# Cached attention with a dense layer, one decode step: K and V of the third step in halves, FFN and part of the output projection in column tiles, unused products in loops

## The chip, the core and the metric

The kernel runs on one core of a Trainium2 chip, in one launch. The metric is the device time of one execution in microseconds (us); of several executions the median counts. A core has a matrix engine (TensorE, PE in the profile; its weight loads are PEld), VectorE (DVE), ScalarE (ACT), GpSimd (POOL) and SyncE (SP), which here issues nearly all DMA transfers. Sixteen DMA engines move the data from HBM to on-chip memory. Engines wait for one another with semaphores.

## The reference

```python
x = A_x                                   # [2, 1, 512], bf16
xn = _layernorm(x)
q = (xn @ wq) -> [2, 32, 1, 128]          # wq [512, 4096]
scores = einsum("bhqd,bhkd->bhqk", q, k_cache) * 128 ** -0.5    # k_cache [2, 32, 8192, 128]
p = softmax(scores)
o = einsum("bhqk,bhkd->bhqd", p, v_cache) # v_cache [2, 32, 8192, 128]
attention = o -> [2, 1, 4096] @ wo        # wo [4096, 512]
ffn = maximum(xn @ w1, 0) @ w2            # w1 [512, 1792], w2 [1792, 512]
return x + attention + ffn
```

(The arrows stand for reshapes.) The inputs are bf16. The two caches hold 268 MB, the weights 12 MB; each element is used once. Two rows of x are all that is multiplied with them.

## The kernel before

The 64 pairs of batch and head are worked on four at a time, in 16 steps (`NP`). A step has one tile of K and one of V, each 128 partitions by 32,768 bf16 elements, 8.39 MB. There is one buffer for each, `ks` and `vs`. A partition holds 256 rows of the cache (`KB`) of one pair; four pairs share the 128 partitions.

In each step TensorE does the following. It transposes the 256 blocks of K (128 by 128), in 32 groups of eight (L275). Each group goes into one of four PSUM tiles `tp` and is copied by VectorE or ScalarE into `kT` (L429). Then come 256 small products of `kT` with the four queries `q4` (L282), which give the scores in `Sc`. VectorE finds a maximum for each half of them (L476, L483), with help of two small products (`turn`, L294, and `spread`, L300). ScalarE makes the exponentials `prm` and their sums (L550). Then come 256 products of V with `prm` (L335), here called PV. After that TensorE runs `WARM` = 24 products whose results nobody uses (L346), in the steps 0 to 13.

The order of the loads is written out by hand on SyncE (L184 to L188): K of step t, V of step t, K of step t+1, and so on. A tile is loaded when its buffer is free: K of the next step after the last transpose of this one (semaphores `pT`), V of the next step after the last product with this V (`sW`). For steps named in `KSPLIT` and `VSPLIT` the tile comes as two DMAs of half the columns, each of which waits only for its own half of the buffer:

```python
c = slice(i * SLOT // 2, (i + 1) * SLOT // 2) if split else slice(0, SLOT)
sp.dma_start(tile[:, c], src[rows, c]).then_inc(d[i], 16)
...
KSPLIT = (0, NP - 1)
VSPLIT = (1, NP - 1)
```

Each half has its own semaphore, `dK[0]` and `dK[1]`, `dV[0]` and `dV[1]`. Where a tile comes whole, GpSimd waits for the first and raises the second (L239). wq lies in `vs` before V, and the query path (layer norm, L254 to L264) runs ahead of the loop.

After the last transpose of the last step, SyncE loads w1, w2 and wo into `ks` (L190 to L194), wo in four pieces of 18, 8, 4 and 2 of its 32 rows (`cuts`; a "row" is here 128 partitions by 512 columns). The tail after the loop is this. TensorE sums the softmax denominators (L356, fp32). It adds x into an accumulator `fin` of 128 partitions by 8 (L362). It forms the FFN's hidden layer in 56 products with two columns, w1 being the stationary operand (L373). VectorE scales and adds the two halves of PV (L494 to L512). TensorE rearranges them (L385, L389), and VectorE copies the result to `OX` (L522). Then `project` (L400) adds w2 times the hidden layer in 56 products and wo times `OX` in 128, all into `fin`, each with w2 or wo as the stationary operand and two moving columns. Each piece of wo is waited for. The end is a copy, a transpose (L420), a copy and the store.

## Time and profile before

| what | value |
|---|---|
| median of 5 executions | 660.07 us (659.49 to 660.3) |
| the profiled execution | 660.29 us |
| its span, first to last instruction | 658.4 us |
| TensorE products busy | 594.6 us, 90% of the span |
| TensorE weight loads busy | 537.3 us, 82% |
| VectorE / ScalarE busy | 261.9 us, 40% / 290.9 us, 44% |
| DMA moved | 280.66 MB, mean 426 GB/s |
| mean granted TensorE clock | 0.98 |

The profile is of one execution. The span leaves out 1.9 us that the time of that execution has besides. All points in time are us from the span's start. The "chain that ended last" is followed back from the last instruction: at each step to whatever released it. "DMA" in it is a wait for a load, from its issue to its landing. An engine's busy time is no measure of what bounds the kernel; the unused products alone make TensorE 74.8 us busier.

### The profile page before, as it was taken

Reading aid. Unit: us, or ns where it says so; the run is one execution under the profiler, and the core shown is the slowest. Engines: PE = TensorE matmul, PEld = TensorE weight load, DVE = VectorE, ACT = ScalarE, POOL = GpSimd, SP = SyncE. Lnnn points to the kernel's source line nnn. Section 1 sums busy time; section 2 is a strip of 40 time slices with the busy share of each in tenths; the row PEclk is TensorE's granted clock in tenths of the full one; section 3 lists DMA queues with packets and bytes.
Section 4 is the critical chain, followed back from the end, with each engine's and each line's share of the span. In section 5 each row is a group of like instructions: output and inputs, shape, how many; then the busy total and the mean of one; then the engine's idle time right before and its main releaser. Section 6 shows DMA issues by size and latency. Waiting matters only on the chain.

```text
span 658.4 us, 27600 instructions
## 1 busy us (share of the span) xinstructions
PE 594.6 (90%) x12987; PEld 537.3 (82%) x12987; DVE 261.9 (40%) x503; ACT 290.9 (44%) x532; POOL 7.1 (1%) x30
## 2 busy tenths in 40 slices
PE   1886999999999999999989999998999999999997
PEld 0585887988879798887969878796987879798986
DVE  1440351716235071633507153260715416071721
ACT  1332443636345263543527354353735435372820
POOL 2000000000000000000000000000000000000000
PEclk9988999989999999999999999999999999999996
DMA  9999999999999999999999999999999999999996
GB/s 380 445 440 428 403 446 402 434 446 442 418 426 434 442 442 414 434 438 442 426 422 430 446 442 434 418 426 446 442 438 418 422 446 442 442 414 417 436 420 268
DMA packets 6223, 280.66 MB, mean 426 GB/s; under 512 B 706, under 2 KB 708, under 8 KB 964
## 3 DMA queue, kind: packets, MB, share of 16 engines
q1 hardware_dynamic: 6208, 280.50, 98.9%
q8 instruction: 8, 0.13, 0.1%
q14 instruction: 3, 0.02, 0.0%
q10 hardware_dynamic: 4, 0.00, 0.0%
HBM read 280.50 MB, written 0.00 MB: 426 GB/s over the span
## 4 chain that ended last, share of the span: by engine, by line
DMA 53%; PE 44%; issue 1%; DVE 1%; SPq 0%; ACT 0%; ACTq 0%
DMA ks<-in_A_k_cache_dram 49%; PE tp L275 34%; DMA ks<-in_A_wo_dram 4%; PE ot L335 4%; PE Sc L282 4%; PE ms L346 2%; DVE mcol L476 1%; SPq L194 0%; ACT L429 0%; PE ms L294 0%; ACT kT L429 0%; PE ms L300 0%; SPq L191 0%; SPq L182 0%; SPq L170 0%
## 5 line engine op out<-in xcount | busy, mean ns | idle before, releaser
L429 DVE COPY kT<-tp 128x1024 bf16<-128x1024 bf16 x320 | 209.3, 688 | 249.2 <-PE tp L275 243.6
L275 PEld LDWEIGHTS tp<-identb,ks 128*128 128x128 bf16 x4096 | 230.4, 98 | 24.7 <-DMA ks<-in_A_k_cache_dram 22.6
L275 PE MATMUL tp<-identb,ks 128*128 128x128 bf16 x4096 | 233.4, 220 | 17.5 <-DMA ks<-in_A_k_cache_dram 16.0
L429 ACT COPY kT<-tp 128x1024 bf16<-128x1024 bf16 x192 | 188.2, 1014 | 129.5 <-PE tp L275 129.5
L282 PE MATMUL Sc<-q,kT 128*128 128x64 bf16 (+8 forms) x4096 | 133.8, 191 | 3.1 <-issue 3.1
L335 PE MATMUL ot<-prm,vs 128*128 128x64 bf16 x4096 | 131.9, 193 | 3.0 <-issue 3.0
L282 PEld LDWEIGHTS Sc<-q,kT 128*128 128x128 bf16 x4096 | 129.3, 98 | 4.5 <-issue 3.2
L335 PEld LDWEIGHTS ot<-prm,vs 128*128 128x128 bf16 x4096 | 128.0, 98 | 4.9 <-issue 3.1
L346 PE MATMUL ms<-identb 128*128 128x512 bf16 x336 | 74.8, 379 | 0.0
L476 DVE TENSOR_REDUCE mcol<-Sc 32x1 bf16<-32x128 f32 x128 | 37.0, 289 | 93.1 <-PE Sc L282 91.7
L550 ACT ACTIVATE prm<-Sc,nm 32x128 bf16<-32x128 f32 x128 | 69.0, 539 | 5.4
L545 ACT COPY nm<-ms 128x4 f32<-128x4 f32 x32 | 5.2, 163 | 139.3 <-PE ms L300 139.3
L346 PEld LDWEIGHTS ms<-identb 128*128 128x128 bf16 x336 | 31.9, 98 | 36.4
L561 ACT COPY OTf<-ot 128x8 f32 x16 | 2.7, 166 | 72.4 <-PE ot L335 72.4
L550 ACT ACTIVATION_READ_ACCUMULATOR prm<-Sc,nm x128 | 32.1, 251 | 0.0
L294 PE MATMUL ms<-identb,mcol 128*1 128x128 bf16 x32 | 6.9, 217 | 22.1 <-DVE mcol L476 22.1
L429 ACT ACT_TABLE_LOAD x16 | 20.5, 1283 | 3.6 <-issue 3.5
L294 PEld LDWEIGHTS ms<-identb,mcol 128*1 128x1 bf16 x32 | 2.5, 79 | 23.9 <-issue 23.1
L254 PE MATMUL ot<-vs,xz 128*16 128x512 bf16 x32 | 9.0, 451 | 8.8 <-DMA vs<-in_A_wq_dram 8.8
L254 PEld LDWEIGHTS ot<-vs,xz 128*16 128x16 bf16 x32 | 3.2, 102 | 14.1 <-issue 11.5
L483 DVE TENSOR_REDUCE mx<-ms 1x4 bf16<-1x128 bf16 x32 | 8.9, 278 | 13.7 <-PE ms L294 13.7
L236 POOL COPY q<-qb 128x4 bf16<-128x4 bf16 x16 | 3.0, 186 | 592.0 <-PE Sc L282 573.0
(61 smaller groups left out, 47.5 us busy)
## 6 DMA issues: line engine op xcount, KB each, us to landing
ks<-in_A_k_cache_dram SPq DMA_DIRECT2D x4, 4096.0 KB, 23.0
vs<-in_A_v_cache_dram SPq DMA_DIRECT2D x4, 4096.0 KB, 22.0
vs<-in_A_wq_dram SPq DMA_DIRECT2D x1, 4096.0 KB, 12.3
ks<-in_B_w_dram SPq DMA_DIRECT2D x2, 1792.0 KB, 16.5
ks<-in_A_wo_dram SPq DMA_DIRECT2D x1, 2304.0 KB
ks<-in_A_wo_dram SPq DMA_DIRECT2D x1, 1024.0 KB, 26.4
ks<-in_A_wo_dram SPq DMA_DIRECT2D x1, 512.0 KB, 27.2
ks<-in_A_wo_dram SPq DMA_DIRECT2D x1, 256.0 KB, 27.3
```

Source lines behind the costliest of these rows:

```text
L236: g.tensor_copy(q4[:], qb[:, U * t:U * t + U]).then_inc(sQ1, 1)
L254: i = pe.matmul(qp, lhsT=xz[:, kt, Z - g * Bsz:Z - g * Bsz + QG * Bsz], rhs=vs[:, (kt * QG + g) * 512:(kt * QG + g + 1) * 512], start=(g = ...
L275: t = pe.transpose(tp[e % 4][:, i, :], ks[:, kk * Dh:(kk + 1) * Dh], identb[:])
L282: t = pe.matmul(Sc[:, U * kk:U * (kk + n)], lhsT=kT[e][:, i, :], rhs=rep(q4[:], n), start=True, stop=True,)
L294: pe.transpose(trp[:, i * P:(i + 1) * P], mcol[:, i:i + 1], identb[:]).then_inc(sT, 1)
L335: t = pe.matmul(oh[:, i, :], lhsT=vs[:, kk * Dh:(kk + 1) * Dh], rhs=rep(prm[:, kk, :], REP), start=(first == 0), stop=(first == KB // 2 - 1),)
L346: pe.matmul(ms[:], lhsT=identb[:], rhs=identb[:].rearrange("p (o k) -> p o k", o=1).to_broadcast([P, 4, P]), start=True, stop=True,)
L429: fn(kT[e][:], tp[e % 4][:]).then_inc(kR[e % HG], 1)
L476: m = v.tensor_reduce(out=mcol[own, i:i + 1], in_=S[own, i * KB // 2:(i + 1) * KB // 2, u], axis=AX.X, op=ALU.max,)
L483: v.tensor_reduce(out=mx[:, i, :], in_=trp[:, i * P:(i + 1) * P].rearrange("o (u m) -> o u m", u=U), axis=AX.X, op=ALU.max, negate=True,). ...
L545: a.copy(nm[:, i, :], bc[:, i, :]).then_inc(sN, 1)
L550: x = a.activation(out=prm[own, k, u], in_=S[own, k, u], func=ACTF.Exp, bias=nm[own, i, u:u + 1], scale=1.0, accum_out=RS[own, i, bass.ds( ...
```

## The change

It has three parts.

1. `KSPLIT` and `VSPLIT`: K and V of step 2 (the third) come in halves. V of the last step comes whole.
2. The FFN and the first 18 rows of wo are turned around. The weights are now the moving operand, 512 columns at a time, and the stationary operand has 32 columns, of which two hold data and the others zeros or what happens to lie there and isn't used. The result takes 32 partitions, so four such products fill different 32-partition strips (`CT` = 32, `TC` = 4) of one PSUM tile. The hidden layer `hp` is made in 16 products instead of 56. ScalarE copies it to bf16, four transposes turn it, and VectorE applies the ReLU. w2 takes 14 products instead of 56, the 18 rows of wo 18 instead of 72. The four strips of the sum `y` are copied to `ys` in fp32, and four fp32 products with `sel2` (a 0/1 matrix) add them into `fin`. The other 14 rows of wo go as before; the pieces are now 18, 6, 6 and 2 rows.
3. The unused products stand in loops of five: 20 in step 0, none in step 1, 25 in the steps 2 to 13.

```diff
-WARM = 24
+CT = 32
...
-    cuts = (0, 18, 26, 30, WJ)
+    cuts = (0, 18, 24, 30, WJ)
+    WIDE = 1
-    KSPLIT = (0, NP - 1)
-    VSPLIT = (1, NP - 1)
+    KSPLIT = (0, 2, NP - 1)
+    VSPLIT = (1, 2)
...
+        g.memset(hT[:], 0.0).then_inc(sI, 1)          # GpSimd, before the loop
...
+        g.wait_ge(sS, 2 * NP)                         # GpSimd, after the loop
+        g.memset(OX, 0.0).then_inc(sI, 1)
...
+        def warm(n):
+            with pe.Fori(0, n):
+                for i in range(5):
+                    pe.matmul(ms[:], lhsT=identb[:], rhs=..., start=True, stop=True)
...
             with pe.If_lt(reg, NP - 1):
-                for i in range(WARM):
-                    pe.matmul(ms[:], lhsT=identb[:], rhs=..., start=True, stop=True)
+                with pe.If_ne(reg, 2):
+                    warm(4)
+                    with pe.If_ne(reg, 1):
+                        warm(1)
...
-        for j in range(FJ):
-            for kt in range(KT):
+        for kt in range(KT):
+            for c in range(TC):
                 i = pe.matmul(
-                    hp[:, j, :],
-                    lhsT=w1_v[:, kt, j, :],
-                    rhs=xz[:, kt, Z:Z + Bsz],
+                    tile(hp, c),
+                    lhsT=xz[:, kt, Z:Z + CT],
+                    rhs=w1_v[:, kt, first_j[c]:first_j[c] + QW, :],
...
+        pe.matmul(
+            tile(y, 0), lhsT=identb[0:Bsz, 0:CT], rhs=xsb[:], start=True, stop=False
+        )
...
+        pe.wait_ge(sF, 2)
+        for i in range(QW):
+            t = pe.transpose(tp[3][:, i, :], hb[:, i * P:(i + 1) * P], identb[:])
+        t.then_inc(sF, 1)
...
         for j in range(FJ):
-            project(w2_sb, j, hT)
+            c = j % TC
+            pe.matmul(
+                tile(y, c), lhsT=hT[:, slot[j], :], rhs=w2_sb[:, j, :],
+                start=(0 < j < TC), stop=False,
+            )
         pe.wait_ge(sV, 110)
-        for c in range(NC):
-            pe.wait_ge(*piece[c])
-            for j in range(cuts[c], cuts[c + 1]):
-                t = project(wo_sb, j, OX, j == WJ - 1)
+        for i in range(WIDE):
+            pe.wait_ge(*piece[i])
+            for j in range(cuts[i], cuts[i + 1]):
+                t = pe.matmul(
+                    tile(y, j % TC), lhsT=OX[:, j, :], rhs=wo_sb[:, j, :],
+                    start=False, stop=(j >= cuts[WIDE] - TC),
+                )
+        t.then_inc(sH, 1)
+        for i in range(WIDE, NC):
+            if i == WIDE:
+                pe.wait_ge(sF, 5)
+                for k in range(KT):
+                    pe.matmul(
+                        fin[:, k * Bsz:(k + 1) * Bsz],
+                        lhsT=ys[:, k * P:(k + 1) * P],
+                        rhs=sel2[:],
+                        start=(k == 0),
+                        stop=False,
+                    )
+            pe.wait_ge(*piece[i])
+            ...                                       # 14 rows, four products each, as before
...
+        v.wait_ge(sF, 3)                              # VectorE
+        v.wait_ge(sI, 4 + U)
+        v.tensor_scalar(out=hT[...], in0=tp[3][...], scalar1=0.0, scalar2=None, op0=ALU.max).then_inc(sF, 1)
...
+        v.wait_ge(sH, 4)
+        v.tensor_copy(ys, y).then_inc(sF, 1)
...
+        a.wait_ge(sF, 1)                              # ScalarE, at the end
+        a.copy(hb, hp).then_inc(sF, 1)
```

## The prediction

> **What bounds the kernel now.** I read the page's DMA queues first, then the chain that ended last, then the tail's timeline and the landings in the trace (sixteen per load, one for each DMA engine; I quote the last).

> ```profile
> q1 hardware_dynamic: 6208, 280.50, 98.9%
> q8 instruction: 8, 0.13, 0.1%
> ```

> The queues are full: 280.50 MB can't move faster than the stream runs. From step 3 on one 8.39 MB tile lands every 19.36 us and a step is 38.70 us. So gains can come only from the start, from holes in the stream, and from what follows the last landing.

> ```profile
> 69.59 5.18 PE ms L346 x24
> 74.77 14.31 PE tp L275 x256
> 89.08 0.01 issue
> 89.09 23.36 DMA ks<-in_A_k_cache_dram
> ...
> 146.25 5.18 PE ms L346 x24
> 151.43 0.03 issue
> 151.45 14.48 PE tp L275 x256
> 165.93 0.02 issue
> 165.95 24.19 DMA ks<-in_A_k_cache_dram
> ...
> 627.41 27.32 DMA ks<-in_A_wo_dram
> 654.73 0.05 issue
> 654.78 0.39 PE Sc L400 x8
> ```

> The chain (start, duration) shows a hole. K of the third step (K2) is issued at 89.09, when all of K1 is transposed, and the second half of V1 lands at 92.34: a lead of 3.25 us. K2 lands at 112.46, 20.12 after V1, so 0.77 beyond 19.36. In later steps the lead is 4.85 (K issued 165.95, V landing 170.80) and costs nothing. So the need lies between; 3.25 + 0.77 = 4.02 is my estimate.

> ```profile
> 650.50 2.06 PE L400 MATMUL Sc<-OX,ks 128*128 128x2 bf16 x72 [0.22 <-DMA ks<-in_A_wo_dram]
> 652.91 0.93 PEld L400 LDWEIGHTS Sc<-OX,ks 128*128 128x128 bf16 x32 [0.43 <-DMA ks<-in_A_wo_dram]
> ```

> In the tail TensorE waits for each piece of wo. The first lands at 650.37 on one engine, 649.56 on the next latest: an instruction packet (q8) sat on an engine from 646.99 for 1.07 us. The end is thus 654.73 plus 3.7 us of product, copies, store and closing, span 658.4. The profiled execution took 660.29, the median 660.07, so I add differences to the median.

> **Halves of K2 and V2.** K2's first half is issued after sixteen groups of K1: warm-up products are now 20 in step 0 (0.86 less), transposes start at 73.9, half of 14.31 later is 81.1, and the second half goes at 88.2. V1 lands at 92.34, so the hole goes: -0.77. Two more issues on SyncE (0.33 to 0.44 each) find it waiting. V2's halves are issued at about 102 and 106, with K2 landing until 111.7: nothing. V15 goes back to one load, after all of PV14 (609.6, before 605.7 for its first half); K15 lands until 615.97, so no hole, but PV15, which began at 634.85, must wait for 635.41: +0.5 for TensorE. The w1 issue behind it waits for 625.1 anyway. GpSimd forwards V15's semaphore and no longer K2's and V2's; it idles 592 us before its copies.

> **Where that stall goes.** Step 1 has no warm-up now. K2's first half lands at 102.1, PV1 ends at about 106.1, TensorE goes straight on; with the table load on ScalarE in the way this takes 15.5 as for K15 (609.6 to 625.1), to 121.9. Then 17.9 of scores and PV (89.08 to 106.97) to 139.8, and 25 products of 0.215 to 145.2. K3 can't land before 111.70 + 38.72 = 150.4: 5 us idle. After pauses of 2.5 to 3 us this trace grants half clock:

> ```profile
> 33.00:34.50 1.50, 0.55 (x9) 0.55 (x10) 0.00 (x0) 0.00 (x0) 0.00 (x0) 0.97 1.41 612
> 34.50:36.00 1.50, 1.50 (x17) 1.50 (x15) 0.50 (x1) 1.01 (x1) 0.00 (x0) 0.50 0.30 131
> 36.00:37.50 1.50, 1.50 (x17) 1.50 (x16) 0.88 (x2) 0.29 (x1) 0.00 (x0) 0.50 1.51 655
> 37.50:39.00 1.50, 1.50 (x27) 1.50 (x26) 0.78 (x2) 1.25 (x2) 0.00 (x0) 0.89 0.30 131
> ```

> (Columns: stretch, length, TensorE, weight load, VectorE, ScalarE, GpSimd, clock, DMA share, GB/s.) 17 transposes per 1.5 us instead of 27 to 30; the 128 took 8.95 instead of 7.24, so 1.71 is lost. In step 3 that makes K4's lead 4.85 - 1.71 = 3.14, and the need of 4.02 then costs 0.88. Ends: 0 (the clock stays) to 1.7 (cold twice as long). I take 0.88, by the K2 row; net of the first hole +0.1. The stall moves by two steps.

> **Loops for the unused products.** Steps from 2 on run 25, not 24: 0.215 more, under a wait of 16.0 us in 13 (1.2 a step) for K. Each pass of a loop costs the sequencer ten instructions and a jump; 48 such instructions were issued in 1.84 us, a taken branch is recorded with 0.20, a register operation with 0.07, so 0.7 against 1.08 us of five products: hidden. Were it not, up to 0.2 a pass still fits the wait; beyond, every step would be late. [...]

> **Shorter code.** TensorE ran dry at 48.43 after 961 of its records and at 62.69 after 1473: 512 records for two 16 KB packets, so edges at 1728, 1984, 2240. The code has 2,234 records. Of the products 4+56+56+72 go and 1+16+4+14+18 come, and eight passes for the fp32 four (L356 shows x8 for four): 127 pairs, 254 records, and some 20 from the loops: about 1,961, under 1984. Before, two packets came in the tail. If none comes, the first wo piece lands at 649.56 and the last at 653.85: -0.8. If one is fetched ahead anyway: 0. I take -0.8.

> **Column tiles.** Their price is open. The nearest row:

> ```profile
> L254 PE MATMUL ot<-vs,xz 128*16 128x512 bf16 x32 | 9.0, 451 | 8.8 <-DMA vs<-in_A_wq_dram 8.8
> ```

> These followed each other every 0.43 us at half clock and 0.215 at full clock, all in one column group, weight loads (102 ns) hidden. Four groups together can't beat a quarter of that; one after another they would take all of it. I take side by side, since all four differ in columns: per group five of the 18 wo products, 1.25 us with the pipeline at full clock, 2.3 at half. [...]

> The tail from PV15 (643.4 with its 0.5): fp32 sums 1.07, FFN products to 645.6 or 646.4, ScalarE's copy 0.6 (half of the 1.01 for 1024 columns), four transposes, ReLU at 648.0, w2 until 649.0 or 650.0. Before, w2 began at 648.63. New waits: TensorE waits for ScalarE's copy, with the products for OX queued behind, VectorE for the transposes, with OX's copy queued behind its ReLU (OX 648.3, before 648.97), and TensorE for the copied sum, with all later wo pieces queued behind: that one is on the path and stands in the sum below. So the wo products begin at 649.7 (649.56 + 0.1), or 650.0 at half clock. Then: products 1.25 / 2.3, copy of 512 fp32 columns 0.68 (L458) + 0.1, fp32 products 1.07 (L356) + 0.1, and 56 products of 28.6 ns (2.06 / 72) = 1.6. Sum 4.8 / 5.85, end at 654.5 / 655.85; the last landing alone would allow 653.95 + 0.44. Before it was 655.17. So -0.7 at full clock, +0.7 at half. The tail from 645.4 ran at half clock before; the wide products are just what raises the clock. Middle: 0.

> Hidden by their covers: the reduction for sel2 (0.2 us ahead of the statistics; the q path waits until 13.28, 8.4 us), memsets on GpSimd (0.5 and 0.95, idle until 24.1 and after 633).

> **Forecast: no change within 0.2% (1.3 us, about what a measurement of this kernel can tell), 0.45.** 660.07 + 0 = 660.0; own range 658.8 to 661.3.

> **Rivals.**
> Faster, 0.27: K4 finds its lead (clock restored in time), so -0.77 and 0.2 of V2's late landing stay, the code packets vanish (-0.9), full clock: 658.3. For it: both holes are real rows. Against: 5 us idle ahead of K3.
> Slower, 0.13: column tiles run one after another. FFN 16 x 0.215 = 3.4, w2 3.0, wo 3.9: the chain ends at 659.9, +4.7, 664.8; at half clock 672. It decides from a speed-up below about three at half clock, two at full. For: no row shows two at once. Against: disjoint columns.
> Slower, 0.15: all does as said, but the packet stays on the wo load, the tail is cold, and K4's lead loses 1.7 (net +0.9): products begin at 651.3, + 5.85 = 657.2, +2.0: 662.1.

> **How the numbers follow.** Faster 0.27, same 0.45, slower 0.28. The range from 658.2 to 662.4 leaves out the serial tiles (0.13) and some edges.

> **What would show it.** K2 landing at 111.7, half clock about 150 with K3's transposes near 16 us, K4 landing 20.2 after V3; no or one q8 packet after 640; eighteen wo products in 1.3 to 2.3 us, and the chain ending in L-lines of the fp32 products rather than in DMA. Wrong, if wide products start 0.2 us or more apart, if TensorE no longer waits for K in steps 5 to 13, or if K4 lands on time.

## The result, and the profile after

The changed kernel is slower, by little: 661.0 us median of 40 runs (659.83 to 664.75) against 659.63 us of 78 runs of the kernel before. The ratio is 1.0024, 95% [1.0015, 1.0032], so some 1.6 us (the medians alone give 1.4); that is just over 0.2%, though the interval reaches below it. The forecast was no change, 660.0 us; 661.0 lies inside its range of times, but against the kernel before the change is larger than the 0.2% it allowed.

The two profiled executions don't show the difference: 660.22 us after, 0.8 below its kernel's median, and 660.29 before, 0.7 above; both have a span of 658.4. They do show where time was won and given back. The page of the profile after, the DMA queue of instructions:

```profile
q8 instruction: 7, 0.11, 0.1%
```

One packet of 16 KB fewer, but one of the seven still starts at 647.62, during the load of wo.

The chain that ended last, after (start, duration; around K of the fourth step, K3, and then the tail):

```profile
122.39 28.18 DMA ks<-in_A_k_cache_dram
150.56 0.05 issue
150.61 17.28 PE tp L289 x256
...
205.48 23.54 DMA ks<-in_A_k_cache_dram
...
609.75 25.71 DMA vs<-in_A_v_cache_dram
...
644.64 3.77 PE tp L389 x16
...
649.75 1.04 PE tp L425 x14
650.79 1.10 PE tp L433 x18
651.91 0.70 DVE kT L576
652.66 1.05 PE Sc L442 x8
653.71 1.47 PE Sc L452 x56
```

K3's transposes take 17.28, where before they took 14.48. From the landing of V15 the chain is now TensorE and the copies between its products to the end, not the DMA of wo.

The timeline after, around step 2 and K4's issue (the bracket is the idle time ahead of a group):

```profile
140.07 5.56 PE L321 MATMUL ms<-identb 128*128 128x512 bf16 x25
150.61 17.28 PE L289 MATMUL tp<-identb,ks 128*128 128x128 bf16 x256 [4.99 <-DMA ks<-in_A_k_cache_dram]
167.92 0.33 SPq L193 DMA_DIRECT2D ks<-in_A_k_cache_dram  x1
```

The windows after (stretch, length, TensorE, weight load, VectorE, ScalarE, GpSimd, clock, DMA share, GB/s):

```profile
148.00:150.50 2.50, 0.00 (x0) 0.00 (x0) 0.00 (x0) 0.00 (x0) 0.00 (x0) 0.84 1.09 472
150.50:154.00 3.50, 3.39 (x32) 3.39 (x33) 1.30 (x2) 1.01 (x1) 0.00 (x0) 0.50 0.99 431
154.00:157.50 3.50, 3.50 (x43) 3.50 (x42) 1.51 (x4) 2.03 (x2) 0.00 (x0) 0.64 0.95 412
```

Before, in the middle one of these stretches (K3 began at 151.45):

```profile
150.50:154.00 3.50, 3.48 (x51) 2.75 (x49) 1.40 (x3) 1.56 (x2) 0.00 (x0) 1.00 0.78 337
```

After the change TensorE is idle for 4.99 us, and the clock is halved from 149.7 to 156.5, which is two stretches of 3.41. So K4 goes out at 167.92, only 1.99 ahead of the last landing of V3 at 169.91; before, the lead was 4.85.

| last landing, us | before | after |
|---|---|---|
| K2 | 112.46 | 111.78 |
| K3 | 151.40 | 150.56 |
| K4, after V3 | 19.34 | 20.05 |
| V4, after K4 | 19.34 | 19.74 |
| V15 | 635.41 | 635.47 |
| 18 rows of wo | 650.37 | 650.39 |
| last piece of wo | 654.73 | 654.76 |

The 0.84 won by K3 is given back entirely at K4 and V4 (0.69 + 0.38). From there on the stream is within 0.3 us of where it was.

### The profile page after: what moved, and what is told of

Its sections match the earlier page's. It is cut to its first block, busy times and chain, and to the rows that moved or that the text cites. A ratio compares the mean times of both kernels' runs of the same rounds, so it can differ in the third digit from the quotient of the medians.

```text
span 658.4 us, 27499 instructions
## 1 busy us (share of the span) xinstructions
PE 592.1 (90%) x12844; PEld 532.5 (81%) x12844; DVE 262.8 (40%) x505; ACT 291.5 (44%) x533; POOL 8.6 (1%) x32
## 3 DMA queue, kind: packets, MB, share of 16 engines
q1 hardware_dynamic: 6352, 280.50, 98.8%
HBM read 280.50 MB, written 0.00 MB: 426 GB/s over the span
## 4 chain that ended last, share of the span: by engine, by line
DMA 54%; PE 44%; DVE 1%; ACT 0%; issue 0%; SPq 0%; ACTq 0%
DMA ks<-in_A_k_cache_dram 50%; PE tp L289 32%; PE ot L358 5%; DMA vs<-in_A_v_cache_dram 4%; PE Sc L296 4%; PE ms L321 1%; PE tp L389 1%; DVE mcol L523 1%; PE Sc L452 0%; ACT L470 0%; PE tp L433 0%; PE ms L308 0%; PE Sc L442 0%; PE tp L425 0%; ACT kT L470 0%
## 5 line engine op out<-in xcount | busy, mean ns | idle before, releaser
L289 PEld LDWEIGHTS tp<-identb,ks 128*128 128x128 bf16 x4096 | 233.2, 99 | 26.5 <-DMA ks<-in_A_k_cache_dram 23.8
L289 PE MATMUL tp<-identb,ks 128*128 128x128 bf16 x4096 | 236.3, 221 | 19.5 <-DMA ks<-in_A_k_cache_dram 17.1
L321 PE MATMUL ms<-identb 128*128 128x512 bf16 x320 | 71.2, 379 | 0.0
L321 PEld LDWEIGHTS ms<-identb 128*128 128x128 bf16 x320 | 30.4, 98 | 34.7
```

The costliest lines, as they stand in the source:

```text
L289: t = pe.transpose(tp[e % 4][:, i, :], ks[:, kk * Dh:(kk + 1) * Dh], identb[:])
L321: pe.matmul(ms[:], lhsT=identb[:], rhs=identb[:].rearrange("p (o k) -> p o k", o=1).to_broadcast([P, 4, P]), start=True, stop=True,)
```

## The experiments

Each ratio is against 35 runs of the kernel before on the same chip (medians 660.19, 659.93 and 659.94 us on the three chips used). The first four share a chip: one half of the change, the other half, the suspected idle time filled in the changed kernel, and the same idle time made in the kernel before.

**loop_part_only**: the kernel before with parts 1 and 3 of the change, and its own tail.

```diff
-    KSPLIT = (0, NP - 1)
-    VSPLIT = (1, NP - 1)
+    KSPLIT = (0, 2, NP - 1)
+    VSPLIT = (1, 2)
-                for i in range(WARM):
-                    pe.matmul(ms[:], ...)
+                with pe.If_ne(reg, 2):
+                    warm(4)
+                    with pe.If_ne(reg, 1):
+                        warm(1)
```

> Before with the halves of K2 and V2, V15 whole, and the unused products in loops (20, none, 25); the tail stays as before. Theory 1, the stall that moved to the fourth step costs the time: this is about as slow as the full change, ratio to before 1.002, and K4 lands 20 us or more after V3 (19.36 would be the stream). Theory 2, the new tail costs it: this is no slower than before, ratio 0.999 to 1.000. Theory 3, V15 as one load costs it (0.5 us at PV15): the last wo piece lands no later than before and the end is about 0.1% later.

Measured: 661.4 us, ratio 1.0018 [1.0006, 1.0029]. Its timeline:

```profile
138.38 5.56 PE L306 MATMUL ms<-identb 128*128 128x512 bf16 x25
150.42 16.51 PE L274 MATMUL tp<-identb,ks 128*128 128x128 bf16 x256 [6.48 <-DMA ks<-in_A_k_cache_dram]
```

K4 is issued at 166.96 and lands 20.88 after V3, 1.52 too late. Half the change is enough for the loss. The stream isn't all of it in this execution: the last piece of wo lands at 655.11, 0.4 later than before, but the chain ends at 656.39, 1.2 later, because TensorE ran late. PV of the last step starts later than before (first line: before) and finds half clock from 636.0 to 639.4:

```profile
634.85 1.14 PE L335 MATMUL ot<-prm,vs 128*128 128x64 bf16 x32
636.19 1.89 PE L343 MATMUL ot<-prm,vs 128*128 128x64 bf16 x32 [0.42 <-DMA vs<-in_A_v_cache_dram]
```

Half clock there is in tail_part_only and step2_filled too (granted clock 0.67 and 0.64 from 634 to 638), which are no slower than before, so it alone isn't the cause; what it adds when the stream is late stays open.

**tail_part_only**: the changed kernel with the splits and the 24 unrolled products of before, so part 2 alone.

```diff
-    KSPLIT = (0, 2, NP - 1)
-    VSPLIT = (1, 2)
+    KSPLIT = (0, NP - 1)
+    VSPLIT = (1, NP - 1)
-                with pe.If_ne(reg, 2):
-                    warm(4)
-                    with pe.If_ne(reg, 1):
-                        warm(1)
+                for i in range(24):
+                    pe.matmul(ms[:], ...)
```

> Before with the new tail alone (FFN and 18 rows of wo in column tiles, pieces 18, 6, 6, 2); splits and the 24 unrolled unused products as before. Theory 1: ratio 0.998 to 1.000, since one instruction packet fewer comes in the tail. Theory 2: ratio 1.002, with the chain ending in the FFN products, the copy of the sum and the fp32 products, and not in the DMA. Its wide w1 products should again take 0.9 us per four (3.8 us in all), w2 and wo 0.215 per four at full clock.

Measured: 659.93 us, ratio 1.0001 [0.9989, 1.0013], span 658.4, one packet in the tail at 647.3. The tail neither gains nor loses. Here K2 lands only 0.31 late (before's profile: 0.77), with the same splits as before.

**step2_filled**: the changed kernel with 20 more unused products in step 2, so that TensorE stays busy until K3 lands.

```diff
                     with pe.If_ne(reg, 1):
                         warm(1)
+                    with pe.If_eq(reg, 3):
+                        warm(4)
```

> The changed kernel with 20 more unused products in step 2, 45 instead of 25, which reach to where K3 lands. Theory 1: the clock stays at full speed at K3, its transposes take 14.5 instead of 17.3 us, K4 is issued 2.8 us earlier and lands 19.4 after V3 instead of 20.05; all later landings come 0.7 to 1.1 us earlier, ratio to before 0.999 to 1.000 (from 1.0024). Theory 2: the landings move as said but the end stays, ratio 1.002.

Measured: 660.14 us, ratio 0.9999 [0.9989, 1.0009]. The windows and the timeline of it:

```profile
150.50:154.00 3.50, 3.45 (x62) 3.46 (x63) 2.10 (x4) 2.47 (x3) 0.00 (x0) 1.00 0.95 412
```

```profile
138.65 9.87 PE L321 MATMUL ms<-identb 128*128 128x512 bf16 x45
150.55 14.47 PE L289 MATMUL tp<-identb,ks 128*128 128x128 bf16 x256 [2.02 <-DMA ks<-in_A_k_cache_dram]
```

62 transposes in 3.5 us, not 32; the clock is full, K3's transposes take 14.47 again, and K4 lands 19.35 after V3. Twenty products that compute nothing take the loss away, with the new tail and V15 as one load still in place, so neither of these is the loss by itself. The last landing comes 1.5 us earlier than in the changed kernel (653.22), but this execution doesn't get that: V15 is one load, PV15 ran at half clock from 635.1 to 638.5, and the chain of the tail ended at 655.45.

**step2_cold**: the kernel before, without its 24 unused products in step 2 and otherwise untouched.

```diff
+                with pe.If_ne(reg, 3):
                     for i in range(WARM):
                         pe.matmul(ms[:], ...)
```

> Before, without the 24 unused products in step 2 alone: TensorE waits 5 to 6 us for K3 there and nothing else changes. Theory 1: half clock at K3, its transposes take 16 to 17.3 us, K4 lands up to 1 us late, ratio 1.001 to 1.002, with a wider spread of times. Theory 2: the transposes are slower but the lead of K4 (4.9 us) still covers it, ratio 1.000.

Measured: 661.65 us, ratio 1.0023 [1.0008, 1.0037]. Its timeline:

```profile
150.35 16.66 PE L275 MATMUL tp<-identb,ks 128*128 128x128 bf16 x256 [6.36 <-DMA ks<-in_A_k_cache_dram]
167.03 0.33 SPq L182 DMA_DIRECT2D ks<-in_A_k_cache_dram  x1
```

K4 lands 21.47 after V3, 2.1 late, and the last piece of wo at 655.80. So idle time ahead of K3 (6.36 us here) costs as much as the measured loss without any other part of the change.

The others ask whether a version can keep K2's gain and be faster than the kernel before.

**filled_v15_halves**: step2_filled, and V15 in halves again.

```diff
-    VSPLIT = (1, 2)
+    VSPLIT = (1, 2, NP - 1)
```

> The changed kernel with 20 more unused products in step 2 and V15 in halves again. If V15 as one load is what holds the tail (theory 3), PV15 starts about 0.5 us earlier and the last chain ends 0.5 us earlier: ratio 0.998 to 0.999. If the tail is held by the chain from the FFN products on, whatever V15 does (theory 2 within a stream that no longer stalls): PV15's end moves by less than 0.3 us and the ratio is 0.999 to 1.000.

Measured: 659.58 us, ratio 0.9996 [0.9983, 1.0008]; no difference from the kernel before. In its profiled execution 45 products didn't keep the clock:

```profile
138.43 9.87 PE L321 MATMUL ms<-identb 128*128 128x512 bf16 x45
150.46 16.09 PE L289 MATMUL tp<-identb,ks 128*128 128x128 bf16 x256 [2.15 <-DMA ks<-in_A_k_cache_dram]
```

With 2.15 us of idle the clock fell (151.4 to 154.8) and K4 came 1.15 late. With 2.02 in step2_filled it stayed, but so it did with 2.14 in filled_w1_near and in filled_old_tail (both below), which have the same 45 products; this is filled_old_tail:

```profile
150.52 14.47 PE L274 MATMUL tp<-identb,ks 128*128 128x128 bf16 x256 [2.14 <-DMA ks<-in_A_k_cache_dram]
```

So it isn't the length of the idle time that parts them; the last section works out what does.

**filled_w1_near** and **filled_w1_row**: the same, with w1's and w2's rows laid out so that the moving columns of a w1 product lie 2 elements apart (`b` = 2) or next to each other (`b` = 1) instead of 14. w2 then comes in pieces of 2 KB or 1 KB.

```diff
-        sp.dma_start(w2_sb, B_w2.rearrange("(p j) n -> p j n", j=FJ))
+        sp.dma_start(
+            w2_sb.rearrange("p (a b) n -> p a (b n)", b=b),
+            B_w2.rearrange("(a p b) n -> p a (b n)", b=b, p=P),
+        )
...
-        w1_v = w1_sb.rearrange("p kt (f j) -> p kt j f", j=FJ)
+        w1_v = w1_sb.rearrange("p kt (a f b) -> p kt a b f", b=b, f=P)
...
-                    rhs=w1_v[:, kt, first_j[c]:first_j[c] + QW, :],
+                    rhs=w1_v[:, kt, first_j[c] // b:(first_j[c] + QW) // b, :, :],
```

> As filled_v15_halves, with another order of the hidden layer: w1's moving columns lie 2 elements apart instead of 14, and w2 is loaded in 2 KB pieces instead of 14 KB. If the 0.9 us per four wide w1 products come from the distance of the columns, they take 0.22 to 0.45 per four here and the chain before the wo products shortens by 1.9 to 2.7 us; the end is then given by the last landing, 1 to 1.5 us earlier: ratio 0.997 to 0.998. If it comes from something else (the four strips of one bank, the loads), they stay at 0.9 and the ratio is as in filled_v15_halves. If the 2 KB pieces slow the load, w2 takes longer than 4.3 us from w1's landing and eats the gain.

> As filled_w1_near, with w1's moving columns next to each other and w2 loaded in 1 KB pieces. By the distance theory 0.215 per four, as w2's and wo's products; the load of w2 is the open price, 4.3 us (none) to 6 us.

Measured: 661.84 us, ratio 1.0028 [1.0014, 1.0042], and 662.68 us, 1.0046 [1.003, 1.0063]: slower than filled_v15_halves, though the w1 products became 3.5 times faster. The timeline of filled_w1_near:

```profile
642.95 1.09 PE L394 MATMUL tp<-ks,xz 128*32 128x512 bf16 x16
649.20 1.26 PE L438 MATMUL tp<-ks,kT 128*32 128x512 bf16 x18 [2.10 <-DMA ks<-in_A_wo_dram]
651.24 1.87 PE L447 MATMUL Sc<-sel,kT 128*128 128x2 f32 x8 [0.78 <-DVE kT L581]
```

What TensorE saves in the hidden layer it waits for wo (2.10), and after that wait the clock is half: the fp32 products take 1.87 instead of 1.05. (This execution, 660.01 us, is the fastest of its twelve.) w2 takes 4.71 us to load (5.21 with 1 KB), not 4.28. In filled_w1_row's execution TensorE waits 1.56 for wo, but the clock stays full in these products, and it is the slowest kernel of all:

```profile
653.46 1.05 PE L447 MATMUL Sc<-sel,kT 128*128 128x2 f32 x8 [0.78 <-DVE kT L581]
```

So half clock in the last products isn't all that makes these kernels slower.

**w1_row_w2_as_before** parts the order of w1's columns from w2's pieces: filled_v15_halves with w1's columns adjacent and w2 loaded as before.

```diff
-                    rhs=w1_v[:, kt, first_j[c]:first_j[c] + QW, :],
+                    rhs=w1_sb[:, kt, first_j[c] * P:(first_j[c] + QW) * P],
```

> As filled_v15_halves, with w1's moving columns next to each other and w2 loaded as before (the hidden layer's order is then mixed up: the FFN's sum is not the reference's). It tells apart why the versions with the other order of the hidden layer were slower. If the small pieces of w2 cost it: ratio 0.997 to 0.999 here, the wide w1 products at 0.215 per four. If it is the idle TensorE that follows short FFN products (half clock in the last products): ratio 1.002, as in filled_w1_near.

Measured: 661.57 us, ratio 1.0026 [1.0012, 1.004], about 2.0 above filled_v15_halves. So w2's pieces aren't needed for the loss. The timeline:

```profile
644.80 1.05 PE L391 MATMUL tp<-ks,xz 128*32 128x512 bf16 x16
650.87 1.26 PE L435 MATMUL tp<-ks,kT 128*32 128x512 bf16 x18 [1.93 <-DMA ks<-in_A_wo_dram]
652.91 1.86 PE L444 MATMUL Sc<-sel,kT 128*128 128x2 f32 x8 [0.78 <-DVE kT L578]
```

The same wait and the same half clock: 0.8 of the 2.0 is seen here. The 18 rows of wo also land 0.45 later than in filled_v15_halves (650.73, 650.28). The rest stays open.

**filled_old_tail** and **filled50_old_tail**: loop_part_only with V15 in halves and 45 or 50 products in step 2, so K2's gain with the old tail.

```diff
-    VSPLIT = (1, 2)
+    VSPLIT = (1, 2, NP - 1)
+                    with pe.If_eq(reg, 3):
+                        warm(4)          # warm(5) for 50
```

> Before with the halves of K2 and V2 and the loops, 20 more unused products in step 2, V15 in halves, and the tail of before: the stalls are gone, the tail is unchanged. The landings come as in step2_filled, 1 to 1.5 us before those of before. If the old tail follows its DMA, ratio 0.998; if two instruction packets in the tail and the PE chain hold it, 0.999 to 1.000, no better than the new tail.

> As filled_old_tail with 50 unused products in step 2 instead of 45, so that they reach K3's landing even when step 2 runs early. Theory 1 (the clock at K3): half clock at K3 becomes rarer, K4 lands 19.4 after V3; ratio 0.998 to 0.999 and a narrower spread. If 45 was enough already: as filled_old_tail, 0.999.

Measured: 659.60 us, ratio 0.9992 [0.9976, 1.0007], and 659.48 us, 0.9998 [0.9982, 1.0013]. K4 lands 19.34 and 19.35 after V3, and the last piece of wo at 653.30 and 653.12; the profiled spans are 657.8 and 657.3, against 658.4. With the next kernel's 657.4 these are the three shortest, yet the intervals hold 1. Both intervals lie below that of the changed kernel.

**filled50_v15_halves**: filled_v15_halves with 50.

> As filled_v15_halves with 50 unused products in step 2; there the profiled run still fell to half clock at K3. Theory 1: K3's transposes 14.5 us, K4 19.4 after V3, ratio 0.998 to 0.999.

Measured: 660.33 us, ratio 1.0011 [1.0, 1.0022], though the profiled span is 657.4 and K4 is in time (19.34). No better than the old tail.

**k2_halves_alone**: the kernel before with one edit.

```diff
-    KSPLIT = (0, NP - 1)
+    KSPLIT = (0, 2, NP - 1)
```

> Before with K of the third step in halves and nothing else: V15 in halves, 24 unrolled unused products in every step, so the hole ahead of K2 is closed and no new wait is made. If the hole is as large as in the profiled run (0.77 us), ratio 0.999; K2 lands 19.4 after V1. If the hole varies from run to run (0 to 0.8), 0.9995 to 1.000.

Measured: 660.19 us, ratio 1.0002 [0.9985, 1.0019]. Its timeline:

```profile
142.81 5.34 PE L346 MATMUL ms<-identb 128*128 128x512 bf16 x24
150.33 16.09 PE L275 MATMUL tp<-identb,ks 128*128 128x128 bf16 x256 [2.17 <-DMA ks<-in_A_k_cache_dram]
```

K2 lands 19.43 after V1, so the hole of 0.77 is gone, and the time doesn't move. Even with step 1's unused products in place, TensorE is now early in step 2 (2.17 idle) and the clock falls, so this run doesn't show the gain by itself. K4, issued 3.18 ahead, landed in time in this execution.

## Why the prediction was wrong, point by point

**The step that failed is the balance of the stream: "net of the first hole +0.1".** Its mechanism was right and is shown from both sides: idle ahead of K3, half clock, K4 issued late, a hole (step2_cold makes it, 1.0023; step2_filled removes it, 0.9999). Both terms were mis-sized.

- The gain, -0.77, was one execution's. The same K2 load, whole as before, was late by 0.31 in tail_part_only and by nothing in step2_cold. k2_halves_alone removes it for a ratio of 1.0002, with a cold K3 of its own; filled_old_tail and filled50_old_tail, with K3 warm in their profiles, come to 0.9992 and 0.9998. By the traces it was worth some 0 to 0.8, and I booked the top.
- The cost, 0.88, came from a lead of 3.14 and one cold stretch of 1.71. Measured: 2.80 more in the transposes (two cold stretches), K4's lead 1.99, and 0.69 + 0.38 late; 1.52 in loop_part_only and 2.1 in step2_cold. My upper end, "1.7 (cold twice as long)", lies among these; the value I took lies below all of them. Two cold stretches is what the prediction put at the end of its span and not into its sum.
- "Need 4.02" isn't a number of the chip: a lead of 4.20 cost 0.31 (tail_part_only), 3.25 cost 0.77, 3.19 cost 1.15 (filled_v15_halves), 3.18 cost nothing (k2_halves_alone), 2.62 cost 2.1, 1.99 cost 1.07 over two loads. So the same lead, close to the predicted 3.14, cost nothing or 1.15. The sixteen landings of K4 lie 1.93 us apart in the profile before (188.21 to 190.14) and 0.75 in the one after (189.21 to 189.96); what part that has I didn't separate.

A cost of 1.1 to 2.1 (the three traces with a long idle time ahead of K3) less a gain of 0 to 0.8 is 0.3 to 2.1, and the measured 1.6 lies in it.

**Idle time before K3.** Predicted 5, measured 4.99; K2 at 111.7, measured 111.78. This part of the walk through step 1 held.

**The packet.** I took -0.8. One packet stayed in the tail, and wo's first 18 rows landed at 650.39 (before: 650.37). The alternative, "fetched ahead anyway: 0", is what happened. By the prediction's own edges, an estimate from two stalls of TensorE (48.43 and 62.69), this was due: 1,961 records reach past 1728, so one of the two packets of the tail remains. What a packet costs isn't shown either: from w1's last landing to that of wo's 18 rows it took 9.81 us in step2_filled and 11.21 in tail_part_only, each with one packet (647.71 and 647.3).

**Column tiles.** Side by side, as taken: four products of w2 start within 10 ns of each other, and the next four 0.215 us later; wo's start in pairs, four in some 0.22 us. The groups after (busy us, mean ns of one):

```profile
L389 PE MATMUL tp<-ks,xz 128*32 128x512 bf16 x16 | 3.8, 1086 | 0.0
L433 PE MATMUL tp<-ks,kT 128*32 128x512 bf16 x18 | 1.3, 380 | 0.0
L425 PE MATMUL tp<-ks,hT 128*32 128x512 bf16 x14 | 1.0, 382 | 0.1
```

wo's 18 took 1.34 (predicted 1.25), the copy 0.69, the fp32 products 1.05, the last 56 products 1.60. All four tiles use all 128 rows, and their weight loads are hidden: wo's 18 loads of 96 ns each, 1.73 us one after another, lie within the 1.34. The clock, which before was half from 645.39 on, stayed full here until 654.89, so the sum at full clock was the one that applied. Missed was L389: a w1 product takes 1086 ns, its columns being 14 bf16 elements (28 bytes) apart, and the sixteen take 3.81 us; at a distance of 2 elements the same sixteen took 1.09 us in all (filled_w1_near), adjacent 1.05 (w1_row_w2_as_before). Why the distance costs this isn't shown. The hidden layer so ended at 648.4, not 645.6, and wo's products began at 650.53, not 649.7; the copy, transposes and ReLU between took 1.3, where the prediction had 2.4. It cost next to nothing, since wo's 18 rows landed only at 650.39. From there 4.7 us (4.8 summed) lead to 655.20; before, the chain ended at 655.19. "Middle: 0" was right by luck: two misses, the packet and the stride, met at the same time. The other sum, 5.85 at half clock, was too small by 0.8: it kept the fp32 products at 1.07, and at half clock they took 1.87 (filled_w1_near).

**Loops.** Hidden, as taken: passes of five follow each other without a gap the trace shows (25 products in 5.56 us, 24 unrolled ones in 5.34), nothing in steps 5 to 13 moved, and no packet of instructions (q8) starts between 70.48 and 647.62.

**Chances.** The loss was a case that I gave 0.15 with a warm stream as its rival; "K4's lead loses 1.7" was in it, tied to a cold tail, which isn't needed. The stream's cost should have stood as a rival by itself, with the K2 gain between 0 and 0.77. The prediction has two ranges, 658.8 to 661.3 beside the forecast and 658.2 to 662.4 under the chances; 661.0 lies in both.

## What to carry to other kernels

A load that is issued when an engine has finished was here only as punctual as that engine's clock (K3's transposes 2.80 us longer, K4's lead 1.99 instead of 4.85): before taking unused work away or making a step earlier, follow TensorE to its next wait, and price what the half clock after it does to the next issue. A gap seen in one execution is a sample; look for the same gap in other executions before booking its full size. Where two chains end within 0.2 us of each other, as the tail's two did here, shortening one alone bought nothing (w1's products 2.7 us shorter in filled_w1_near, ratio 1.0028), and TensorE, which then waited 1.56 to 2.10 us, ran the fp32 products of the tail at half clock in two of three traces (1.87 and 1.86 us instead of 1.05).
